# Row maxima and sums of an attention kernel: partition groups joined by scalar copies and a vector transpose instead of a TensorE transpose

## The chip, the cores and the metric

The kernel runs on one core of one Trainium2 chip. The metric is the device time of one execution in microseconds (us), the median of several runs. The core has TensorE (PE, matrix products; PEld is its weight load), VectorE (DVE), ScalarE (ACT), GpSimd (POOL) and SyncE (SP), which here only issues DMAs. Each engine runs its own instructions in order; they wait for each other by semaphores.

## The reference

```python
xn = layernorm(x)                                  # x: 2048 x 640
q  = (xn @ wq) in 32 heads of 128
s  = softmax(q @ k.T * 128**-0.5) @ v              # the last 512 keys of a cache, per head
s  = (heads side by side) @ wo                     # 2048 x 640
h  = relu(xn @ w1 + b1) ** 2                       # 640 -> 1728
g  = silu(h @ w2 + b2)
out = x + s * g
```

All is float32. Products are made from a high and a low part of each operand (fp32r), three matmuls for each product.

## The kernel before, in words

The 2048 rows are four tiles of 512. First the gate `g` is computed for three of the tiles (lines up to about 350; roughly the first 300 us). Then attention runs in 128 **units**: 32 heads times 4 row tiles. The gate of the last tile is mixed into the first and last units.

In a unit the scores lie transposed: keys on the 128 partitions, the 512 rows of x along the free dimension, in four chunks of 128 keys (`KC`), two chunks to a PSUM tile `s` of 128x1024. A unit goes through these steps:

- `s_mm`: 12 matmuls give the scores, in two tiles `s`. There are two such buffers, so the next unit's scores wait until this unit's have been read.
- `max_fold`: VectorE reads 128x1024 scores, transposes each square of 32x32 and takes the maximum over 32 keys (`fold`, group `rdm<-s`). Afterwards partition 32a + i holds maxima over the 32 keys of partition group a, for row 32b + i in column b, for each of the four chunks: 128x64.
- `gather` (`r1m<-rdm`): the maximum over the chunks, 128x16. `turn` (`ptm`): a TensorE transpose against the identity, to a PSUM tile of 16x128. `row` (`rowm<-ptm`): the maximum over the four partition groups a, now along the free dimension, 16x32: one value for each of the 512 rows. Then two DMAs from SP's queue: the row to DRAM (`m_d<-rowm`, 2 KB) and back to all 128 partitions (`bm<-m_d`, 256 KB).
- `shift` (`e<-s,bm`): scores less maxima, on VectorE; this frees the two `s` buffers. `expo` and `p_hi` on ScalarE, `p_lo` and `s_add` on GpSimd: the exponentials, their split in two parts (`pt`), and the sum of the two halves (`su`).
- `s_fold`, `gather`, `turn`, `row` once more for the sums (`rds`, `r1s`, `pts`, `rows`, a reciprocal, `s_d`, `bs`), one unit later.
- `v_mm` (`o<-pt,wv`, 12 matmuls), `o_norm` (times the reciprocal, `o<-o,bs`), `o_hi` and `o_lo` (`ot`). After two heads, `r_mm` (15 matmuls a unit on average) and `r_acc` (`acc<-r,acc`) for the projection by `wo`. `q_mm` (`pq`, 15 matmuls), `q_hi` and `q_lo` make the q of two units ahead. `prep` splits the weights.

The order of the work is written out by hand: a plan gives every step a time within its unit, steps are sorted by these times, and that is the order of the instructions on every engine. The times are used for nothing else.

```python
PERIOD = 12.4
for when, k, f, a in sorted(plan, key=lambda e: e[:2]):
    f(*a)
```

`late_square` squares the activations of the last tile's gate on GpSimd; three of its calls, in the first three units, are planned in the loop over `range(FA, FC)`.

Of the kernel before, what the change touches and what calls it, by code (L numbers as in the profile page):

```python
# [20 lines left out]
def kernel(  # L21
# [21 lines left out]
    FC = (F + P - 1) // P  # L43
    KC = W // P
# [7 lines left out]
    cpool = ctx.enter_context(tc.tile_pool(name="const", bufs=1))  # L52
    dpool = ctx.enter_context(tc.tile_pool(name="dram", bufs=1, space=bass.MemoryType.DRAM))

    ident = cpool.tile([P, P], F32, name="ident")
# [8 lines left out]
    class Ordered:  # L64
# [13 lines left out]
    pe, dve, act, pool, sp = (  # L78
        Ordered(e) for e in (nc.tensor, nc.vector, nc.scalar, nc.gpsimd, nc.sync)
    )  # L80
# [18 lines left out]
    psx = ctx.enter_context(tc.tile_pool(name="psx", bufs=1, space=PSUM))  # L99

    FA = FC - 3
# [76 lines left out]
    def ln_rows(t, mv, xs):  # L178
        pm = psx.tile([P, NT], F32, tag="x", name=f"pmv{t}")
        nc.tensor.transpose(pm[: 2 * NB, :P], mv.rearrange("p a b -> p (a b)"), ident)  # L180
        row = xp.tile([2 * NB, P], F32, tag="lr", name=f"lr{t}", bufs=1)
        nc.vector.tensor_copy(row, pm[: 2 * NB, :P])
        d = dpool.tile([2, NT], F32, name=f"mv_d{t}")
        nc.sync.dma_start(d.rearrange("a (b p) -> (a b) p", p=P), row)
        bc = []
        for i in range(2):
            m = xp.tile([P, D], F32, tag="mr", name=f"mr{t}_{i}")[:, :NT]
            nc.sync.dma_start(m, d[i : i + 1, :].to_broadcast([P, NT]))
            bc.append(m)
        return bc, xs  # L190
# [136 lines left out]
    def mlp_step(n):  # L327
# [47 lines left out]
    PERIOD = 12.4  # L375
    B32 = 32
    AHEAD = 2
    NQ = NT // B32
# [4 lines left out]
    XT, ACC, KT, VV, WQ, WO, Q, E, SC, MB, RD, PT, PO, OT, RB, QPS, FX, CL, PRS, RAW = (  # L383
        {} for _ in range(20)
    )
# [82 lines left out]
    def fold(rd, k, src, op):  # L468
        dve.tensor_reduce(
            rd[:, k * NQ * 2 : (k + 1) * NQ * 2],  # L470
            src.rearrange("p c (b i) -> p (c b) i", i=B32),
            axis=AX.X,
            op=op,
            apply_transpose=True,
        )

    def max_fold(i, k):
        if k == 0:
            RD[i, "m"] = ap.tile([P, KC * NQ], F32, tag="rd", name=f"rdm{i}", bufs=3)
        fold(RD[i, "m"], k, SC[i, k], ALU.max)  # L480

    def gather(i, what):
        rd = RD.pop((i, what))
        n = rd.shape[1] // NQ
        r1 = ap.tile([P, NQ], F32, tag="r1", name=f"r1{what}{i}", bufs=4)
        dve.tensor_reduce(
            r1,
            rd.rearrange("p (c b) -> p b c", b=NQ),
            axis=AX.X,
            op=ALU.max if what == "m" else ALU.add,  # L490
        )
        RD[i, what] = r1

    def turn(i, what):
        pm = psx.tile([P, NT], F32, tag="x", name=f"pt{what}{i}")
        pe.transpose(pm[:NQ, :P], RD.pop((i, what)), ident)
        RD[i, what] = pm

    def row(i, what):
        pm = RD.pop((i, what))  # L500
        r = ap.tile([NQ, B32], F32, tag="row", name=f"row{what}{i}", bufs=4)
        dve.tensor_reduce(
            r,
            pm[:NQ, :P].rearrange("p (a i) -> p i a", i=B32),
            axis=AX.X,
            op=ALU.max if what == "m" else ALU.add,
        )
        if what == "s":
            dve.reciprocal(r, r)
        d = dpool.tile([NQ, B32], F32, tag=f"{what}_d", name=f"{what}_d{i}", bufs=4)  # L510
        sp.dma_start(d, r)
        bc = ap.tile([P, NT], F32, tag=f"b{what}", name=f"b{what}{i}", bufs=2)
        sp.dma_start(bc, d.rearrange("a b -> (a b)")[None, :].to_broadcast([P, NT]))
        (MB if what == "m" else RB)[i] = bc
# [25 lines left out]
        pool.tensor_tensor(RD[i, "su"], E[i, 0], E[i, 1], op=ALU.add)  # L540

    def s_fold(i):
        RD[i, "s"] = ap.tile([P, 2 * NQ], F32, tag="rd", name=f"rds{i}", bufs=3)
        fold(RD[i, "s"], 0, RD.pop((i, "su")), ALU.add)

    def v_mm(i, c):
        hf, g, t, h = units[i]
# [75 lines left out]
    LW, LH, LPH, LPY, LR = {}, {}, {}, {}, {}  # L623
# [98 lines left out]
        else:  # L722
            act.activation(r, ph, AF.Relu, bias=bias)

    def late_square(f):
        pool.tensor_tensor(LR[f], LR[f], LR[f], op=ALU.mult)

    def late_split(f):
        n = chunks[f][1]
# [83 lines left out]
    ap = ctx.enter_context(tc.tile_pool(name="at", bufs=2))  # L813
    pools["psb"] = ctx.enter_context(tc.tile_pool(name="psb", bufs=1, space=PSUM))

    plan = []

    def at(when, f, *a):
        plan.append((max(when, 0.0), len(plan), f, a))
# [16 lines left out]
    for t in range(TPH):  # L836
        for c in range(DC):
            k, late = divmod(c + 1 - t, 2)
# [17 lines left out]
    for i in range(NU):  # L856
        t0 = i * PERIOD

        def on(when, f, *a):
            at(t0 + when, f, *a)  # L860

        hf, g, t, h = units[i]
        for c in range(KC):
            on(0.68 * c, s_mm, i, c)
        if i + AHEAD < NU:
            q_at = 3.45 if i % G and i > UPG else 4.3
            for c in range(DC):
                on(q_at + 0.68 * c, q_mm, i + AHEAD, (c,))
            on(q_at + 3.5, q_hi, i + AHEAD)
            on(q_at + 4.1, q_lo, i + AHEAD)  # L870
        on(1.4, max_fold, i, 0)
        on(2.8, max_fold, i, 1)
        on(3.95, gather, i, "m")
        on(5.0, turn, i, "m")
        on(5.4, row, i, "m")
        on(10.4, shift, i, 0)
        on(11.6, shift, i, 1)
        on(11.7, expo, i, 0)
        on(12.7, p_hi, i, 0)
        on(13.8, expo, i, 1)  # L880
        on(14.8, p_hi, i, 1)
        on(13.9, p_lo, i, 0)
        on(16.2, s_add, i)
        on(PERIOD + 6.2, s_fold, i)
        on(PERIOD + 7.4, gather, i, "s")
        on(PERIOD + (8.45 if i < FC - FA - 1 else 9.2), turn, i, "s")
        on(PERIOD + 9.6, row, i, "s")
        on(18.6, p_lo, i, 1)
        for c in range(KC):
            on(PERIOD + 8.5 + 0.68 * c, v_mm, i, c)  # L890
        on(2 * PERIOD + 4.2, o_norm, i)
        on(2 * PERIOD + 4.9, o_hi, i)
        on(2 * PERIOD + 5.5, o_lo, i)
        if i % G == G - 1:
            for d in range(DC):
                last = i == NU - G - 1
                if i < NU - 1:
                    for when, js in (R_AT_END if last else R_AT)[d]:
                        on(when, r_mm, i, d, js, (R_BANK_END if last else R_BANK)[d])
                    on(when + 0.68 * len(js), r_acc, i, d)  # L900
                if g == NG - 1 and hf == 0:
                    w = (NU // 2 + 9 + 4 * (t * DC + d)) * PERIOD
                    for k, n in enumerate("sxg"):
                        at(w + k * PERIOD - 0.6, load_finish, n, 0, t, d)
                    at(w + 3 * PERIOD - 0.7, finish, 0, t, d)
# [10 lines left out]
    for item in order:  # L916
        kind, n = item[0], int(item[1:] or 0)
# [37 lines left out]
    for f, u in sorted(UP_AT.items()):  # L955
        at(LOAD.get(f, PREP.get(f - 2, 0) + 0.9), late_load, 1, f)
        when = PREP.setdefault(f, u - 5.0)
        at(when, late_prep, 1, f)
        for c in range(DC):
            at(u + 0.68 * c, late_up, f, UP_BANK[f] if f < len(UP_BANK) else (f + 1) % 2, c)  # L960
        relu, square, split = STEPS_AT.get(f, (u + 3.5, u + 4.3, u + 5.7))
        at(relu, late_relu, f, "kv"[f % 2])
        at(square, late_square, f)
        at(split, late_split, f)
# [8 lines left out]
    for k, f in enumerate(range(FA, FC)):  # L973
        t0 = k * PERIOD
        for c in range(DC):
            at(t0 + 8.0 + 0.1 * c, early_up, f, 0, c)
        at(t0 + 10.6, late_relu, f, "s")
        at(t0 + 12.0, late_square, f)
        at(t0 + PERIOD + 7.6, early_split, f)
    at(z + 2.0, late_x)  # L980
    for d in range(DC):
# [51 lines left out]
```

## Time and profile before

| | us |
|---|---|
| median of 3 runs | 2020.71 (2017.9 to 2021.19) |
| profiled execution | 2021.47 |
| its span in the trace | 2019.7 |
| granted TensorE clock | 0.999 of full speed |

In the trace every line of this part of the kernel carries the number of one helper (L72), so instructions are told apart by the names of what they write and read: `rdm<-s` writes `rdm` and reads `s`. A row of a timeline has start, length, engine, operation, and in brackets the idle time before it and what ended it. A group has the busy time in all, the mean in ns of one, and the idle time before. SPq is the sequencer that issues DMAs from SP.

### The profile page before, as it was taken

The page shows a single profiled execution, that of the slowest core. Times are in us where ns is not written, and L with a number is a line of the kernel's source. Part 1 is how long each engine was busy: PE and PEld are TensorE (multiplying, and loading weights), DVE is VectorE, ACT ScalarE, POOL GpSimd, SP SyncE. Part 2 cuts the span into 40 slices and gives each one's busy share as a digit, 9 for nine tenths or more (in the row PEclk, how much of TensorE's full clock was granted, in tenths as well). Part 3 has the DMA queues.
Part 4 walks back from the last instruction along what each step waited for, and adds up shares of the span by engine and source line. Part 5 has one row for each costly group of instructions (what it writes and reads, how often), then busy time and mean ns, then how long its engine had stood idle before and what let it go on. Part 6 is the DMA issues. An engine that isn't in the chain of part 4 may idle for free.

```text
span 2019.7 us, 25025 instructions
## 1 busy us (share of the span) xinstructions
PE 1987.9 (98%) x8832; PEld 1609.3 (80%) x8832; DVE 1535.8 (76%) x2252; ACT 985.8 (49%) x1266; POOL 1375.4 (68%) x754
## 2 busy tenths in 40 slices
PE   7999999999999999999999999999999999999998
PEld 6788887788888888888887788787878888788877
DVE  5532337788888888888887778888888888888864
ACT  4432335555555555555554455555555555555533
POOL 1121227788777777777777788788888888877841
PEclk9999999999999999999999999999999999999999
DMA  4431454322333332333335433333333333333344
GB/s 140 128 113 29 177 196 132 99 90 89 90 89 89 90 89 90 90 91 90 91 96 159 154 95 105 110 110 111 110 110 111 110 112 110 96 91 90 106 146 140
DMA packets 126862, 220.32 MB, mean 109 GB/s; under 512 B 21542, under 2 KB 36304, under 8 KB 125456
## 3 DMA queue, kind: packets, MB, share of 16 engines
q1 hardware_dynamic: 123744, 204.28, 33.6%
q0 software_dynamic: 2992, 14.43, 1.8%
q8 instruction: 70, 1.15, 0.2%
q14 instruction: 56, 0.46, 0.1%
HBM read 194.26 MB, written 24.39 MB: 108 GB/s over the span
## 4 chain that ended last, share of the span: by engine, by line
PE 88%; DMA 6%; DVE 2%; POOL 1%; ACT 1%; issue 1%; SPq 0%; POOLq 0%; DVEq 0%
PE pq L72 20%; PE r L72 19%; PE s L72 17%; PE o L72 15%; DMA bm<-m_d 2%; PE py L96 2%; PE py L97 2%; PE py L95 2%; PE ph L96 2%; PE ph L95 2%; PE ph L97 2%; PE ly L72 2%; DMA m_d<-rowm 1%; PE lu L72 1%; DMA w1r<-in_w_dram 1%; DVE e L72 1%
## 5 line engine op out<-in xcount | busy, mean ns | idle before, releaser
L72 POOL TENSOR_TENSOR pt<-e,pt 128x1024 fp32r<-128x1024 f32 x256 | 617.5, 2412 | 296.1 <-ACT pt L72 296.1
L72 PE MATMUL r<-ot,wo 128*128 128x512 f32 x1920 | 496.9, 389 | 0.5 <-DVE acc L72 0.5
L72 PE MATMUL pq<-ax,wq 128*128 128x512 f32 x1920 | 473.1, 396 | 0.1
L72 ACT ACTIVATE e<-e 128x1024 f32<-128x1024 f32 x256 | 269.5, 1053 | 370.6 <-DVE e L72 331.6
L72 PEld LDWEIGHTS r<-ot,wo 128*128 128x128 f32 x1920 | 360.2, 188 | 75.9 <-DVE acc L72 0.9
L72 PEld LDWEIGHTS pq<-ax,wq 128*128 128x128 f32 x1920 | 350.9, 188 | 84.5 <-DMA ax<-xT_d 0.9
L72 PE MATMUL o<-pt,wv 128*128 128x512 f32 x1536 | 386.5, 398 | 0.4 <-POOL pt L72 0.3
L72 PE MATMUL s<-q,wk 128*128 128x512 f32 x1536 | 372.2, 391 | 9.1 <-DVE e L72 9.0
L72 DVE TRANSPOSE_TENSOR_REDUCE rdm<-s 128x32 f32<-128x1024 f32 x256 | 319.3, 1249 | 60.6 <-PE s L72 46.3
L72 PEld LDWEIGHTS s<-q,wk 128*128 128x128 f32 x1536 | 286.4, 188 | 76.9 <-DVE e L72 16.3
L72 PEld LDWEIGHTS o<-pt,wv 128*128 128x128 f32 x1536 | 278.7, 188 | 70.8 <-POOL pt L72 1.5
L72 DVE TENSOR_TENSOR e<-s,bm 128x1024 f32<-128x1024 f32 x256 | 299.9, 1212 | 37.5 <-DMA bm<-m_d 33.7
L72 POOL TENSOR_TENSOR su<-e,e 128x1024 f32<-128x1024 f32 x128 | 308.5, 2410 | 0.0
L72 ACT ACTIVATE pt<-e 128x1024 fp32r<-128x1024 f32 x256 | 271.7, 1061 | 7.8
L72 DVE TENSOR_TENSOR acc<-r,acc 128x512 f32<-128x512 f32 x300 | 202.5, 675 | 2.8 <-PE r L72 2.8
L237 POOL TENSOR_TENSOR r<-r 128x512 f32<-128x512 f32 (+1 forms) x42 | 44.1, 1049 | 227.5 <-ACT r L278 207.9
L72 ACT ACTIVATE ot<-o 128x512 fp32r<-128x512 f32 x128 | 76.8, 600 | 228.3 <-DVE o L72 228.3
L72 DVE TRANSPOSE_TENSOR_REDUCE rds<-su 128x32 f32<-128x1024 f32 x128 | 158.5, 1239 | 10.7 <-POOL su L72 9.0
L72 ACT ACTIVATE q<-pq 128x512 fp32r<-128x512 f32 x128 | 76.7, 599 | 164.8 <-PE pq L72 164.7
L72 DVE TENSOR_TENSOR ot<-o,ot 128x512 fp32r<-128x512 f32 x128 | 88.5, 691 | 32.0 <-ACT ot L72 32.0
L239 DVE TENSOR_TENSOR h<-r,h 128x512 fp32r<-128x512 f32 (+1 forms) x42 | 29.0, 690 | 107.7 <-ACT h L238 107.6
L72 POOL TENSOR_TENSOR wq<-qr,wq 128x640 fp32r<-128x640 f32 x62 | 98.5, 1588 | 4.0 <-ACT wq L72 2.8
(122 smaller groups left out, 2152.6 us busy)
## 6 DMA issues: line engine op xcount, KB each, us to landing
bm<-m_d SPq DMA_DIRECT2D x128, 256.0 KB, 3.3
bs<-s_d SPq DMA_DIRECT2D x128, 256.0 KB, 4.0
qr<-in_wq_dram SPq DMA_DIRECT2D x64, 320.0 KB, 4.4
or<-in_wo_dram SPq DMA_DIRECT2D x64, 320.0 KB, 4.5
kr<-in_kT_dram SPq DMA_DIRECT2D x64, 256.0 KB, 4.4
vr<-in_v_dram SPq DMA_DIRECT2D x64, 256.0 KB, 4.3
xT_d<-xT POOLq DMA_DIRECT2D x6, 1280.0 KB, 7.5
xb<-in_x_dram SPq DMA_DIRECT2D x16, 320.0 KB, 3.5
```

The lines of the kernel that those rows point to most:

```text
L72: ins = method(*args, **kwargs)
L95: nc.tensor.matmul(ps, ah, bh, start=first and i == 0, stop=False)
L96: nc.tensor.matmul(ps, ah, bl, start=False, stop=False)
L97: nc.tensor.matmul(ps, al, bh, start=False, stop=last and i == n - 1)
L237: nc.gpsimd.tensor_tensor(r, r, r, op=ALU.mult)
L239: nc.vector.tensor_tensor(lo, r, raw(hi), op=ALU.subtract)
```

## The change

The two steps `turn`, the TensorE transposes, are gone. `gather` now copies, on ScalarE, partition groups 1 to 3 of the folded tile beside group 0, so that all lie in partitions 0 to 31: three copies of 32x64 for the maxima, of 32x32 for the sums. `row` reduces over groups and chunks in one VectorE step to 32x16, written into the left half of a 32x32 square that was zeroed once; for the sums the reciprocal is taken there; a VectorE transpose of the square then gives the 16x32 row. The DMAs are as before. `row` is planned earlier (4.45 for 5.4, and 8.5 for 9.6 within the unit). Three early squares of the last tile's gate move from GpSimd to VectorE.

```diff
+    def fold_tile(what, i):
+        n = (KC if what == "m" else 2) * NQ
+        return ap.tile([P, P // B32, n], F32, tag=f"rd{what}", name=f"rd{what}{i}", bufs=2)
...
     def gather(i, what):
-        rd = RD.pop((i, what))
-        n = rd.shape[1] // NQ
-        r1 = ap.tile([P, NQ], F32, tag="r1", name=f"r1{what}{i}", bufs=4)
-        dve.tensor_reduce(
-            r1,
-            rd.rearrange("p (c b) -> p b c", b=NQ),
-            axis=AX.X,
-            op=ALU.max if what == "m" else ALU.add,
-        )
-        RD[i, what] = r1
-
-    def turn(i, what):
-        pm = psx.tile([P, NT], F32, tag="x", name=f"pt{what}{i}")
-        pe.transpose(pm[:NQ, :P], RD.pop((i, what)), ident)
-        RD[i, what] = pm
+        rd = RD[i, what]
+        for a in range(1, P // B32):
+            act.activation(rd[:B32, a, :], rd[a * B32 : (a + 1) * B32, 0, :], AF.Copy)
 
     def row(i, what):
-        pm = RD.pop((i, what))
-        r = ap.tile([NQ, B32], F32, tag="row", name=f"row{what}{i}", bufs=4)
-        dve.tensor_reduce(
-            r,
-            pm[:NQ, :P].rearrange("p (a i) -> p i a", i=B32),
-            axis=AX.X,
-            op=ALU.max if what == "m" else ALU.add,
-        )
+        rd = RD.pop((i, what))[:B32].rearrange("p a (c b) -> p b (a c)", b=NQ)
+        sq = SQ[what, i % 2]
+        dve.tensor_reduce(sq[:, :NQ], rd, axis=AX.X, op=ALU.max if what == "m" else ALU.add)
         if what == "s":
-            dve.reciprocal(r, r)
+            dve.reciprocal(sq[:, :NQ], sq[:, :NQ])
+        r = ap.tile([B32, B32], F32, tag="row", name=f"row{what}{i}", bufs=4)
+        dve.transpose(r, sq)
+        r = r[:NQ]
         d = dpool.tile([NQ, B32], F32, tag=f"{what}_d", name=f"{what}_d{i}", bufs=4)
         sp.dma_start(d, r)
...
-    def late_square(f):
-        pool.tensor_tensor(LR[f], LR[f], LR[f], op=ALU.mult)
+    def late_square(f, eng=pool):
+        eng.tensor_tensor(LR[f], LR[f], LR[f], op=ALU.mult)
...
+    SQ = {
+        (what, k): cpool.tile([B32, B32], F32, name=f"sq{what}{k}") for what in "ms" for k in range(2)
+    }
+    for sq in SQ.values():
+        pool.memset(sq, 0.0)
...
         on(3.95, gather, i, "m")
-        on(5.0, turn, i, "m")
-        on(5.4, row, i, "m")
+        on(4.45, row, i, "m")
...
-        on(PERIOD + 7.4, gather, i, "s")
-        on(PERIOD + (8.45 if i < FC - FA - 1 else 9.2), turn, i, "s")
-        on(PERIOD + 9.6, row, i, "s")
+        on(PERIOD + 8.0, gather, i, "s")
+        on(PERIOD + 8.5, row, i, "s")
...
-        at(t0 + 12.0, late_square, f)
+        at(t0 + 12.0, late_square, f, dve)
```

More of the change, by code (lines that the diff above doesn't have):

```diff
@@ L475, in fold @@
         )
+    def fold_tile(what, i):
+        n = (KC if what == "m" else 2) * NQ
+        return ap.tile([P, P // B32, n], F32, tag=f"rd{what}", name=f"rd{what}{i}", bufs=2)
     def max_fold(i, k):
         if k == 0:
-            RD[i, "m"] = ap.tile([P, KC * NQ], F32, tag="rd", name=f"rdm{i}", bufs=3)
-        fold(RD[i, "m"], k, SC[i, k], ALU.max)
+            RD[i, "m"] = fold_tile("m", i)
+        fold(RD[i, "m"][:, 0, :], k, SC[i, k], ALU.max)
     def gather(i, what):
-        rd = RD.pop((i, what))
-        n = rd.shape[1] // NQ
-        r1 = ap.tile([P, NQ], F32, tag="r1", name=f"r1{what}{i}", bufs=4)
-        dve.tensor_reduce(
-            r1,
-            rd.rearrange("p (c b) -> p b c", b=NQ),
-            axis=AX.X,
-            op=ALU.max if what == "m" else ALU.add,
-        )
-        RD[i, what] = r1
-    def turn(i, what):
-        pm = psx.tile([P, NT], F32, tag="x", name=f"pt{what}{i}")
-        pe.transpose(pm[:NQ, :P], RD.pop((i, what)), ident)
-        RD[i, what] = pm
-    def row(i, what):
-        pm = RD.pop((i, what))
-        r = ap.tile([NQ, B32], F32, tag="row", name=f"row{what}{i}", bufs=4)
-        dve.tensor_reduce(
-            r,
-            pm[:NQ, :P].rearrange("p (a i) -> p i a", i=B32),
-            axis=AX.X,
-            op=ALU.max if what == "m" else ALU.add,
-        )
+        rd = RD[i, what]
+        for a in range(1, P // B32):
+            act.activation(rd[:B32, a, :], rd[a * B32 : (a + 1) * B32, 0, :], AF.Copy)
+    def row(i, what):
+        rd = RD.pop((i, what))[:B32].rearrange("p a (c b) -> p b (a c)", b=NQ)
+        sq = SQ[what, i % 2]
+        dve.tensor_reduce(sq[:, :NQ], rd, axis=AX.X, op=ALU.max if what == "m" else ALU.add)
         if what == "s":
-            dve.reciprocal(r, r)
+            dve.reciprocal(sq[:, :NQ], sq[:, :NQ])
+        r = ap.tile([B32, B32], F32, tag="row", name=f"row{what}{i}", bufs=4)
+        dve.transpose(r, sq)
+        r = r[:NQ]
         d = dpool.tile([NQ, B32], F32, tag=f"{what}_d", name=f"{what}_d{i}", bufs=4)
@@ L542, in s_fold @@
     def s_fold(i):
-        RD[i, "s"] = ap.tile([P, 2 * NQ], F32, tag="rd", name=f"rds{i}", bufs=3)
-        fold(RD[i, "s"], 0, RD.pop((i, "su")), ALU.add)
+        RD[i, "s"] = fold_tile("s", i)
+        fold(RD[i, "s"][:, 0, :], 0, RD.pop((i, "su")), ALU.add)
     def v_mm(i, c):
```

## The prediction

> **What bounds the kernel now.** I read the page first, busy shares and then the chain that ended last.
>
> ```profile
> span 2019.7 us, 25025 instructions
> ...
> PE 1987.9 (98%) x8832; PEld 1609.3 (80%) x8832; DVE 1535.8 (76%) x2252; ACT 985.8 (49%) x1266; POOL 1375.4 (68%) x754
> ...
> PE 88%; DMA 6%; DVE 2%; POOL 1%; ACT 1%; issue 1%; SPq 0%; POOLq 0%; DVEq 0%
> ```
>
> TensorE (PE) is the bound, but 6% of the chain is DMA, so something else ends last in places. To see what, I went to the timeline of one unit in the middle of the run, PE first (start, length, engine, operation).
>
> ```profile
> 682.37 2.88 PE L72 MATMUL s<-q,wk 128*128 128x512 f32 x12
> ...
> 685.09 1.52 PE L72 MATMUL r<-ot,wo 128*128 128x512 f32 x6
> ...
> 687.81 0.27 PE L72 MATMUL ptm<-ident,r1m 128*16 128x128 f32 x1
> ...
> 687.84 2.30 PE L72 MATMUL pq<-ax,wq 128*128 128x512 f32 x9
> ...
> 689.98 0.84 PE L72 MATMUL r<-ot,wo 128*128 128x512 f32 x3
> ...
> 694.86 2.88 PE L72 MATMUL s<-q,wk 128*128 128x512 f32 x12
> ```
>
> From one unit's scores to the next is 694.86 - 682.37 = 12.49 us. Twelve matmuls go out in 685.09 - 682.37 = 2.72 us, 0.2267 each. A unit has 54 of them (15 for q, 12 scores, 12 for P.V, 15 for the output projection): 12.24 us. The other 0.25 us are the unit's two transposes. One can be read: 689.98 - 687.81 = 2.17 us hold nine matmuls (2.04) and `ptm`, so it takes 0.13 us of PE time, though its record says 0.27.
>
> The other ring in a unit runs over VectorE (DVE) and two DMAs: maxima of the scores, their row to DRAM, its broadcast back, the subtraction that frees the score banks. The same unit on DVE, ScalarE (ACT) and the DMA queue (SPq):
>
> ```profile
> 683.93 2.61 DVE L72 TRANSPOSE_TENSOR_REDUCE rdm<-s 128x32 f32<-128x1024 f32 x2 [0.31 <-PE s L72]
> ...
> 685.12 1.06 ACT L72 ACTIVATE pt<-e 128x1024 fp32r<-128x1024 f32 x1
> ...
> 686.57 0.27 DVE L72 TENSOR_REDUCE r1m<-rdm 128x16 f32<-128x64 f32 x1
> ...
> 686.75 0.68 DVE L72 TENSOR_TENSOR acc<-r,acc 128x512 f32<-128x512 f32 x1
> 687.35 0.69 DVE L72 TENSOR_TENSOR o<-o,bs 128x512 f32<-128x512 f32 x1
> ...
> 688.08 0.60 ACT L72 ACTIVATE ot<-o 128x512 fp32r<-128x512 f32 x1 [1.90 <-DVE o L72]
> 688.12 0.28 DVE L72 TENSOR_REDUCE rowm<-ptm 16x32 f32<-16x128 f32 x1
> 688.42 0.33 SPq L72 DMA_DIRECT2D m_d<-rowm  x1
> ...
> 689.76 0.33 SPq L72 DMA_DIRECT2D bm<-m_d  x1
> ...
> 693.15 2.36 DVE L72 TENSOR_TENSOR e<-s,bm 128x1024 f32<-128x1024 f32 x2 [0.17 <-DMA bm<-m_d]
> ...
> 696.42 2.61 DVE L72 TRANSPOSE_TENSOR_REDUCE rdm<-s 128x32 f32<-128x1024 f32 x2 [0.32 <-PE s L72]
> ...
> 698.96 0.65 DVE L72 TENSOR_TENSOR acc<-r,acc 128x512 f32<-128x512 f32 x1
> ```
>
> From the first fold to the end of `rowm`: 688.40 - 683.93 = 4.47 us. From there to `e`: 4.75 us here, and `e` waited for the DMA. The fold that follows at 696.42 waited 0.32 us for PE, so this unit was PE's. A unit whose broadcast came late shows the ring when it alone decides:
>
> ```profile
> 520.73 2.61 DVE L72 TRANSPOSE_TENSOR_REDUCE rdm<-s 128x32 f32<-128x1024 f32 x2 [0.60 <-PE s L72]
> ...
> 524.92 0.28 DVE L72 TENSOR_REDUCE rowm<-ptm 16x32 f32<-16x128 f32 x1 [0.23 <-PE ptm L72]
> ...
> 530.85 2.36 DVE L72 TENSOR_TENSOR e<-s,bm 128x1024 f32<-128x1024 f32 x2 [1.07 <-DMA bm<-m_d]
> ...
> 533.83 2.61 DVE L72 TRANSPOSE_TENSOR_REDUCE rdm<-s 128x32 f32<-128x1024 f32 x2
> ```
>
> Fold to fold 13.10 us: 4.47 to the end of `rowm`, 5.65 to `e`, 2.98 to the next fold, which no longer waits. So the ring takes 7.45 us + d, d being the time from the end of `rowm` to `e`. It decides where d is over 5.04. At the 4.75 of the unit above it takes 12.20: only 0.29 us hide it behind PE's 12.49, and it is just under the 12.24 that PE needs without transposes. This near tie is the whole question. The waits agree that the DMA is late now and then (us in total, times, longest):
>
> ```profile
> DVE e L72 <- DMA bm<-m_d: 33.7, 49, 2.6
> ```
>
> I read d in every unit but the first four and the last, whose surroundings differ: 123 pairs of `rowm` and `e` rows, from the first to the last of these:
>
> ```profile
> 362.48 0.27 DVE L72 TENSOR_REDUCE rowm<-ptm 16x32 f32<-16x128 f32 x1
> ...
> 367.33 2.36 DVE L72 TENSOR_TENSOR e<-s,bm 128x1024 f32<-128x1024 f32 x2 [0.37 <-DMA bm<-m_d]
> ...
> 1901.32 0.28 DVE L72 TENSOR_REDUCE rowm<-ptm 16x32 f32<-16x128 f32 x1
> ...
> 1906.20 2.36 DVE L72 TENSOR_TENSOR e<-s,bm 128x1024 f32<-128x1024 f32 x2
> ```
>
> 77 have d up to 4.72, 24 lie between 4.72 and 5.04 (mean 4.85), and 22 are over 5.04 (mean 5.63): those are the ring's already.
>
> **The change part by part.** Durations of the groups (total busy, then mean ns of one, then idle before):
>
> ```profile
> L72 DVE RECIPROCAL rows<-rows 16x32 f32<-16x32 f32 x128 | 43.7, 341 | 4.4
> ...
> L72 PE MATMUL ptm<-ident,r1m 128*16 128x128 f32 x128 | 34.7, 271 | 1.4 <-DVE r1m L72 1.1 <-issue 0.3
> L72 DVE TENSOR_REDUCE r1m<-rdm 128x16 f32<-128x64 f32 x128 | 33.0, 258 | 2.4
> ...
> L72 DVE TENSOR_REDUCE r1s<-rds 128x16 f32<-128x32 f32 x128 | 24.1, 188 | 4.4
> ...
> L72 DVE TENSOR_TENSOR mv<-sc 128x4 f32<-128x4 f32 x4 | 0.6, 162 | 0.1
> ...
> L72 ACT ACTIVATE wk<-kr 128x512 fp32r<-128x512 f32 x64 | 39.8, 622 | 0.0
> ...
> L154 ACT ACTIVATE sc<-sc 128x4 f32<-128x4 f32 x4 | 0.8, 206 | 2.0 <-DVE sc L72 1.9
> ...
> L72 ACT ACTIVATE e<-e 128x1024 f32<-128x1024 f32 x256 | 269.5, 1053 | 370.6 <-DVE e L72 331.6 <-POOL wk L72 17.1 <-POOL wo L72 15.5
> ```
>
> *PE.* All 256 transposes go. At 0.125 us each that is 32 us, the most the change can give; PE then needs 12.24 us a unit.
>
> *Scalar copies.* Three a join, two joins a unit. From 206 ns at 4 elements and 622 at 512 a copy of 64 is about 255 ns, one of 32 about 230 (estimates). The fold of the maxima ends 2.61 us after its start; ACT takes over 0.04 us later (as `ot` at 688.08 followed `o`, ended at 688.04), and three copies are done at 2.61 + 0.04 + 0.77 = 3.42. ACT is free then: its `pt` ended at 686.18, 2.25 after the fold began. In the changed order DVE runs `acc` and `o` right behind the folds: `acc` goes out 2.54 after the first fold (698.96 - 696.42), `o` 0.60 later (as at 686.75 and 687.35), the joined maximum 0.60 after that, at 3.75. So the copies are hidden, with 0.3 us to spare; without that cover the first 0.3 us cost nothing and each further us costs a us in every unit where the ring decides. Behind them on ACT stand `ot`, which needs `o` anyway, and, behind those of the sums, the weight copies and then the exponentials, before which ACT waits 331.6 us for DVE, 2.6 us a unit: covered.
>
> *The joined reduction.* It reads 256 elements in each of 32 partitions where `r1m` read 64 in 128. At the rate of one element per 0.96 ns that 162 ns for 4 and 188 for 32 give, it is 0.40 us; at the slope from `r1s` to `r1m` (70 ns for 32 elements) 0.68. I take 0.55, the middle, since neither row is near.
>
> The Trainium skill (SBUF - State Buffer, in "Door 1: The DMA port swizzle") has a rule that speaks against this step: SBUF is read in 16-byte lines, and each access in a new line pays a penalty. The elements here lie 64 bytes apart, each in a line of its own. The trace is divided: `r1s` has the same spacing and shows no penalty, `r1m` does. By the rule the sum would be that of the second rival below.
>
> *The turn on VectorE.* 32 elements; no row shows it. It is nearest to `r1s` (188 ns for 32), bounded by 162 and 258: I take 0.20. So `rowm` ends at 3.75 + 0.55 + 0.03 (the gap from `rdm` to `r1m`) + 0.20 = 4.53 instead of 4.47, rounded up with one hand-over more to 0.07 later. With the bounds, 0.13 earlier to 0.25 later.
>
> *The sums.* The same steps, half as wide, off the ring: in the 4.75 us until `e` DVE has `ot`, `q` and at most one more `acc` (0.60 each), a fold (1.30), the join (0.4), a reciprocal (under the 0.34 of 32 elements, it has 16) and the turn (0.2): 4.04. Nothing. The sums' row no longer waits for its place among PE's matmuls, so its two DMAs are issued earlier; they stand behind `bm` on SPq as before.
>
> *Sum.* The ring becomes 7.52 + d. In the 77 units d is at most 4.72, so PE decides: 0.25 each, 19.2 us. In the 24 the period is 7.52 + 4.85 = 12.37, a gain of 0.12 each, 2.9. The 22 late ones lose 0.07 each, 1.5. Together 20.6. The other five units: 1.25 for their transposes and the 1.4 us that PE stood idle before `ptm`, less about 0.5 for each of the first two units, where no `acc` or `o` hides the copies: 1.6. The three early squares that go from GpSimd to DVE I cost at nothing: in the new order each falls before folds that wait for PE, 0.67 us in this row, as long as a square of the size of `acc` takes; uncovered they would be some 2 us.
>
> ```profile
> 332.94 1.25 DVE L72 TRANSPOSE_TENSOR_REDUCE rdm<-s 128x32 f32<-128x1024 f32 x1 [0.67 <-PE s L72]
> ```
>
> 22 us off the profiled execution's 2021.47 us gives 1999.3; that execution is 0.8 above the median of 2020.71, so 1998.5 in its terms; I say 1999.
>
> **The rivals.**
>
> *PE decides nearly everywhere.* If the reduction takes 0.40 us, `rowm` ends 0.05 earlier than now or better, and 90 or more units run at 12.24: 25 to 31 us gained, 1989 to 1995. For it speaks `r1s`; against it, d itself must not grow.
>
> *The ring swallows half of the gain.* With 0.68 us and a turn of 0.2, `rowm` ends 0.20 later; only 32 units have room for PE's 12.24, 69 gain little, and 11 us remain: about 2009. For it speaks the slope to `r1m`. This is what the skill's rule on lines would make of it. Near 0.3 later the gain is used up: no change.
>
> *Slower: the copies are not hidden.* Were they 0.5 us each, hand-overs counted, the join could start only at 2.61 + 0.04 + 1.5 + 0.03 = 4.18, `rowm` would end about 0.5 later, and every unit would be the ring's: some 24 us lost, about 2045. It decides from about 0.43 us a copy. Against it: 206 ns for the smallest ACT row. For it: none of the rows reads one group of partitions and writes another.
>
> The skill (ScalarE: Activation LUTs, "What ACT_TABLE_LOAD costs") gives 186 ns + 0.833 ns an element and says that back-to-back ones overlap by 93 ns; the 622 ns at 512 agree, and three copies would then be some 0.5 us, not 0.77.
>
> That the transposes stay can't be: none is issued any more.
>
> **How the numbers follow.** Forecast (1995 to 2005) 0.45, PE nearly everywhere 0.20, half swallowed (2005 to 2016) 0.18, no change 0.05, slower 0.12. Within 0.2%, 4 us, this kernel can't be told from no change. Faster is 0.45 + 0.20 + 0.18 = 0.83. The range takes in the first three cases, 1989 to 2017, and leaves out the rest.
>
> **What would show it.** Right: PE-bound units 12.24 us apart; `rowm` ending 4.5 to 4.6 after the first fold; the joined maximum not waiting for ACT; more waits of `e` for `bm` (33.7 us in 49 now would rise), for the slack is gone. Wrong: a joined maximum that waits for ACT, or over 0.7 us of reduction; units at 12.4 or more with folds that never wait for PE; a longer d, if the sums' DMAs get in the way of `bm`.

## The result and the profile after

| | before | changed kernel |
|---|---|---|
| median of 4 runs each | 2019.87 us (2017.9 to 2021.19) | 1997.3 us (1995.06 to 1998.71) |
| ratio to before | | 0.9887 [0.9876, 0.9899] |
| profiled execution | 2021.47 | 1995.06 |
| its span | 2019.7 | 1993.3 |

Forecast was 1999. The page of the changed kernel: busy time of the engines, the chain that ended last, and the two groups of scalar copies.

```profile
span 1993.3 us, 25531 instructions
...
PE 1961.8 (98%) x8576; PEld 1601.6 (80%) x8576; DVE 1563.8 (78%) x2255; ACT 1183.6 (59%) x2034; POOL 1374.1 (69%) x755
...
PE 87%; DMA 5%; DVE 4%; POOL 1%; ACT 1%; issue 1%; SPq 0%; DVEq 0%; ACTq 0%; POOLq 0%
...
L72 ACT ACTIVATE rdm<-rdm 32x64 f32<-32x64 f32 x384 | 98.2, 256 | 38.2 <-DVE rdm L72 33.4
L72 ACT ACTIVATE rds<-rds 32x32 f32<-32x32 f32 x384 | 87.6, 228 | 49.4 <-DVE rds L72 45.1
```

PE has 256 instructions fewer (8832 to 8576) and is as full as before. DVE's share of the chain went from 2 to 4%: the second ring is nearer. The copies take 256 and 228 ns.

The medians differ by 22.6 us, this pair of traces by 26.4, since the traced execution of the kernel before is above all four of the table and that of the changed one is the lowest of its four. To see where the 26.4 us of span came from I cut it at the first folds of the fifth and of the last unit, which leaves the 123 periods, from fold to fold, that the prediction counted (worked out from the starts of the folds `rdm<-s`):

| us | before | after | gain |
|---|---|---|---|
| up to the first counted fold | 357.92 | 358.16 | -0.2 |
| 123 periods | 1551.7 | 1525.4 | 26.3 |
| from the last counted fold on | 110.08 | 109.75 | 0.3 |
| PE's floor for them (123 x 12.49, x 12.24) | 1536.3 | 1505.5 | 30.8 |
| over the floor | 15.4 | 19.9 | -4.5 |

So all of it lies in the units: PE gave 30.8 us, and the ring of DVE and DMAs took 4.5 back. The size of the second part hangs on the execution. A second trace of the changed kernel stands 18.7 us over the floor, near the 19.9 here, but the two experiments below that add only a few idle transposes at the start of the kernel before stand 9.9 over it, not 15.4. Two neighbouring units in the timeline of the changed kernel (start, length, engine, operation):

```profile
677.63 3.01 PE L72 MATMUL s<-q,wk 128*128 128x512 f32 x12 [0.36 <-DVE e L72]
...
679.30 2.63 DVE L72 TRANSPOSE_TENSOR_REDUCE rdm<-s 128x32 f32<-128x1024 f32 x2
...
680.48 1.52 PE L72 MATMUL r<-ot,wo 128*128 128x512 f32 x6
...
681.97 0.79 ACT L72 ACTIVATE rdm<-rdm 32x64 f32<-32x64 f32 x3 [0.19 <-DVE rdm L72]
682.04 0.69 DVE L72 TENSOR_TENSOR acc<-r,acc 128x512 f32<-128x512 f32 x1
682.65 0.69 DVE L72 TENSOR_TENSOR o<-o,bs 128x512 f32<-128x512 f32 x1
683.25 0.58 DVE L72 TENSOR_REDUCE sqm<-rdm 32x16 f32<-32x256 f32 x1
683.86 0.20 DVE L72 STREAM_TRANSPOSE rowm<-sqm 32x32 f32<-32x32 f32 x1
...
688.74 2.35 DVE L72 TENSOR_TENSOR e<-s,bm 128x1024 f32<-128x1024 f32 x2 [1.05 <-DMA bm<-m_d]
...
691.77 2.63 DVE L72 TRANSPOSE_TENSOR_REDUCE rdm<-s 128x32 f32<-128x1024 f32 x2
...
694.32 0.65 DVE L72 TENSOR_TENSOR acc<-r,acc 128x512 f32<-128x512 f32 x1
694.43 0.79 ACT L72 ACTIVATE rdm<-rdm 32x64 f32<-32x64 f32 x3 [0.18 <-DVE rdm L72]
...
695.49 0.57 DVE L72 TENSOR_REDUCE sqm<-rdm 32x16 f32<-32x256 f32 x1
696.10 0.20 DVE L72 STREAM_TRANSPOSE rowm<-sqm 32x32 f32<-32x32 f32 x1
```

Three things are to be seen. First, the copies are hidden: they are over at 681.97 + 0.79 = 682.76, 3.46 after the first fold, while DVE is with `o` until 683.34. Second, the two units differ. In the lower one `acc` goes out 694.32 - 691.77 = 2.55 after the first fold, and the row is done at 4.53. In the upper one `acc` starts at 2.74: the six `r` matmuls, whose sum it adds, end only at 680.48 + 1.52 = 682.00. The row is done at 4.76. Third, the ring decides here: the fold at 691.77 has no idle time before it, it comes 12.47 us after the one before, and PE's scores ahead of the first fold waited 0.36 us for `e`.

Over all counted units the row ends 4.74 after the first fold in one half of the units and 4.52 in the other (medians), where it was 4.47 before, and the median periods are 12.39 and 12.27. Only 54 of 123 periods are at most 0.03 over PE's floor, which is called on the floor below; before it was 95.

The joined row's instructions in the changed kernel, one tile at a time (shortest, median, longest in ns, first and last start), with what the reduction of the maxima waited for (us, times), and for the sums:

```profile
L72 DVE TENSOR_REDUCE sqm<-rdm x128: 564/578/617, 311.6 to 1887.3; 32x16 f32<-32x256 f32 x128
L72 DVE STREAM_TRANSPOSE rowm<-sqm x128: 198/199/202, 312.2 to 1887.9; 32x32 f32<-32x32 f32 x128
...
  ACT rdm L72: 5.8, 11
```

```profile
L72 DVE TENSOR_REDUCE sqs<-rds x128: 342/360/379, 329.0 to 1906.4; 32x16 f32<-32x128 f32 x128
L72 DVE RECIPROCAL sqs<-sqs x128: 240/241/244, 329.4 to 1906.7; 32x16 f32<-32x16 f32 x128
```

And the wait that answers to the 33.7 us in 49 of before (us, times, longest):

```profile
DVE e L72 <- DMA bm<-m_d: 99.2, 125, 3.2
```

Now `e` waits for its broadcast in nearly every unit. Yet d, from the row's end to `e`, went over 5.04 in 6 of 123 units and no longer in 22. The prediction took d as given; this had to be explained.

### The profile page after: what moved, and what is told of

The parts are those of the page before. It is cut to its first block, busy times and chain, and to the rows that moved or that the text cites. A ratio compares the mean times of both kernels' runs of the same rounds, so it can differ in the third digit from the quotient of the medians.

```text
span 1993.3 us, 25531 instructions
## 1 busy us (share of the span) xinstructions
PE 1961.8 (98%) x8576; PEld 1601.6 (80%) x8576; DVE 1563.8 (78%) x2255; ACT 1183.6 (59%) x2034; POOL 1374.1 (69%) x755
## 3 DMA queue, kind: packets, MB, share of 16 engines
q1 hardware_dynamic: 123744, 204.28, 33.7%
## 4 chain that ended last, share of the span: by engine, by line
PE 87%; DMA 5%; DVE 4%; POOL 1%; ACT 1%; issue 1%; SPq 0%; DVEq 0%; ACTq 0%; POOLq 0%
PE r L72 20%; PE pq L72 20%; PE s L72 17%; PE o L72 16%; PE ly L72 2%; PE py L96 2%; PE py L97 2%; PE py L95 2%; PE ph L96 2%; PE ph L97 2%; PE ph L95 2%; DMA bm<-m_d 2%; PE lu L72 1%; DMA w1r<-in_w_dram 1%; DMA m_d<-rowm 1%
## 5 line engine op out<-in xcount | busy, mean ns | idle before, releaser
L72 PE MATMUL pq<-ax,wq 128*128 128x512 f32 x1920 | 456.5, 389 | 1.6 <-DMA ax<-xT_d 1.5
L72 PEld LDWEIGHTS pq<-ax,wq 128*128 128x128 f32 x1920 | 360.3, 188 | 77.0 <-DMA ax<-xT_d 2.3
L72 DVE TENSOR_TENSOR e<-s,bm 128x1024 f32<-128x1024 f32 x256 | 301.5, 1219 | 99.3 <-DMA bm<-m_d 99.2
L72 PE MATMUL o<-pt,wv 128*128 128x512 f32 x1536 | 372.1, 390 | 1.4 <-POOL pt L72 0.9
L72 DVE TRANSPOSE_TENSOR_REDUCE rdm<-s 128x32 f32<-128x1024 f32 x256 | 318.9, 1248 | 38.8 <-PE s L72 19.5
L72 PEld LDWEIGHTS o<-pt,wv 128*128 128x128 f32 x1536 | 287.2, 188 | 65.6 <-POOL pt L72 6.1
L72 ACT ACTIVATE rdm<-rdm 32x64 f32<-32x64 f32 x384 | 98.2, 256 | 38.2 <-DVE rdm L72 33.4
L72 ACT ACTIVATE rds<-rds 32x32 f32<-32x32 f32 x384 | 87.6, 228 | 49.4 <-DVE rds L72 45.1
```

The source lines that it names most:

```text
L72: ins = method(*args, **kwargs)
```

## Experiments

Results are given by the median and by the ratio to the kernel before, run on the same chip in the same rounds. "Periods" are the 123 of the table above, and a late row is one whose first DMA (`m_d`) and second (`bm`) are issued over 1.5 us apart. Before had 25 late rows, the changed kernel 7.

**Is the gain PE's time?** The transposes come back, as idle ones that no row waits for.

```diff
+    def turn(i, what):
+        pm = psx.tile([P, NT], F32, tag="x", name=f"pt{what}{i}")
+        pe.transpose(pm[:NQ, :P], ident[:, :NQ], ident)
...
+        on(5.0, turn, i, "m")
...
+        on(PERIOD + (8.45 if i < FC - FA - 1 else 9.2), turn, i, "s")
```

> The changed kernel with the 256 TensorE transposes put back at their old places in PE's order, now of a piece of the identity and read by nobody: PE's time as before, the row's way as after. Theory (PE's time is most of the gain, and rows that arrive late cost more when PE's floor is low): PE needs 12.49 us a unit again, the DVE-DMA ring at 4.53 or 4.76 + 2.98 us + the DMA time of some 4.4 to 4.7 us stays under that, so units run at 12.49 and only a few late ones longer: about 2015 us, +18 on the changed kernel, and some 5 us under the kernel before, because fewer rows come late. Rival (the gain is PE's time alone): 2020, no difference to the kernel before. Rival (the gain is the earlier DMAs of the sums, PE's time is hidden anyway): 2000 or less.

Measured 2015.26 us, ratio 0.998 [0.997, 0.9989]: some 18 of the 22.6 us are gone. Two folds in its timeline and the idle transpose between them:

```profile
686.24 2.61 DVE L72 TRANSPOSE_TENSOR_REDUCE rdm<-s 128x32 f32<-128x1024 f32 x2 [0.33 <-PE s L72]
...
690.12 0.27 PE L72 MATMUL ptm<-ident 128*16 128x128 f32 x1
...
698.73 2.61 DVE L72 TRANSPOSE_TENSOR_REDUCE rdm<-s 128x32 f32<-128x1024 f32 x2 [0.19 <-PE s L72]
```

The folds are 12.49 apart again and wait for PE. 110 of 123 periods are on that floor, though the row ends as late as in the changed kernel (4.74 and 4.51) and no row waits for the transposes. So the gain is the 0.125 us of PE time of each transpose, not the shorter way of the row. The 4 us that stay go with the late rows: 8 here, 25 before, and 6.2 us over the floor where before had 15.4. In the trace of the kernel before, 15.1 of these 15.4 us stand in the 25 periods with a late row.

**Is the rest of the floor held back by the row's end?** `acc` goes behind the row instead of in front of it.

```diff
+                done = when + 0.68 * len(js)
+                if not last and 3.0 < done % PERIOD < 4.5:
+                    done += 4.6 - done % PERIOD
-                on(when + 0.68 * len(js), r_acc, i, d)
+                on(done, r_acc, i, d)
```

> The changed kernel with the output sums (acc) that stand between the folds and the joined maximum on DVE moved behind the row of maxima. Theory (in every second unit acc waits for PE's projection matmuls and holds the joined maximum back, 4.76 us from fold to row instead of 4.53, and the ring decides there): the joined maximum then starts when the three copies are done, 3.48 after the first fold, and the row ends at 4.29 in both kinds of unit; ring 4.29 + 2.98 + d under 12.24 for every d up to 4.97, so all but the late units run at PE's 12.24: 10 to 15 us less than the changed kernel, 1983 to 1987. Rival (the ring is not what holds units at 12.4, but DVE's total work): the same work in another order, no change, 1997. The wait of the joined maximum for ACT should now appear in most units, 0.3 us each.

Measured 1984.74 us, ratio 0.9825 [0.9806, 0.9843], against 0.9887 for the change as it is. DVE in its timeline, and the wait that appeared:

```profile
679.72 2.61 DVE L72 TRANSPOSE_TENSOR_REDUCE rdm<-s 128x32 f32<-128x1024 f32 x2 [0.29 <-PE s L72]
...
682.25 0.67 DVE L72 TENSOR_TENSOR o<-o,bs 128x512 f32<-128x512 f32 x1
...
683.18 0.59 DVE L72 TENSOR_REDUCE sqm<-rdm 32x16 f32<-32x256 f32 x1 [0.27 <-ACT rdm L72]
683.81 0.20 DVE L72 STREAM_TRANSPOSE rowm<-sqm 32x32 f32<-32x32 f32 x1
683.95 0.64 DVE L72 TENSOR_TENSOR acc<-r,acc 128x512 f32<-128x512 f32 x1
...
691.96 2.61 DVE L72 TRANSPOSE_TENSOR_REDUCE rdm<-s 128x32 f32<-128x1024 f32 x2 [0.32 <-PE s L72]
```

```profile
DVE sqm L72 <- ACT rdm L72: 34.7, 126, 1.0
```

The row ends at 4.30 in both halves of the units, 102 of 123 periods are on the floor of 12.24, and the folds wait for PE. The copies now show, by 0.27 us each, and it does not matter. So the changed kernel's loss against PE's floor is a matter of where the row ends, and 0.2 to 0.4 us of that was one accumulation that stood in front of it.

**What if the copies were not hidden?** The three copies of the maxima are made twice: the rival that ended on the other side.

```diff
-        for a in range(1, P // B32):
+        for a in (1, 2, 3) * (2 if what == "m" else 1):
```

> The changed kernel with the three scalar copies of each maximum made twice, six of 0.256 us. Theory (three are hidden behind acc and o, by 0.3 us, and beyond that each us costs a us in the units where the ring decides): the copies end about 2.65 + 1.55 + 0.03 = 4.23 us after the first fold, the joined maximum starts 0.3 to 0.5 us later than now, every unit is the ring's at 12.6 to 12.7: about +30 us, 2024 to 2034, slower than the kernel before. Rival (ACT has time to spare, 59% busy, and the copies stay hidden): within 5 us of 1997.

Measured 2060.46 us, ratio 1.0199 [1.0181, 1.0217]: 63 us over the changed kernel, about twice what I expected. The direction holds, the size was wrong: the ring had been put at 12.6 to 12.7 us, and the first four units took 6 us longer than in the changed kernel besides. Its chain of what ended last, and one unit:

```profile
PE 38%; DMA 26%; DVE 20%; ACT 11%; issue 3%; POOL 2%; SPq 0%; ACTq 0%; DVEq 0%
```

```profile
700.76 2.61 DVE L72 TRANSPOSE_TENSOR_REDUCE rdm<-s 128x32 f32<-128x1024 f32 x2
703.40 1.66 ACT L72 ACTIVATE rdm<-rdm 32x64 f32<-32x64 f32 x6 [0.15 <-DVE rdm L72]
705.09 0.58 DVE L72 TENSOR_REDUCE sqm<-rdm 32x16 f32<-32x256 f32 x1 [0.31 <-ACT rdm L72]
705.71 0.20 DVE L72 STREAM_TRANSPOSE rowm<-sqm 32x32 f32<-32x32 f32 x1
...
710.58 2.35 DVE L72 TENSOR_TENSOR e<-s,bm 128x1024 f32<-128x1024 f32 x2 [1.29 <-DMA bm<-m_d]
...
713.61 2.61 DVE L72 TRANSPOSE_TENSOR_REDUCE rdm<-s 128x32 f32<-128x1024 f32 x2
```

This is the ring alone: row at 5.15, 4.67 to `e`, 3.03 to the next fold, 12.85 us, the median of the units, and 123 x 12.85 = 1581 of the 1583.0 us of its periods. No unit is PE's. It shows how a ring that is off the chain today becomes the chain whole: 0.41 us more on the row in one half of the units, 0.63 in the other, and PE's share of the chain falls from 87 to 38%.

**What does the spacing of the joined reduction cost?** The fold writes in another order, so that the four chunks of a column lie side by side (16 bytes) instead of 64 bytes apart; the copies carry the order along.

```diff
-            rd[:, k * NQ * 2 : (k + 1) * NQ * 2],
-            src.rearrange("p c (b i) -> p (c b) i", i=B32),
+            rd.rearrange("p (b c) -> p c b", b=NQ)[:, 2 * k : 2 * k + 2, :],
+            src.rearrange("p c (b i) -> p c b i", i=B32),
...
-        rd = RD.pop((i, what))[:B32].rearrange("p a (c b) -> p b (a c)", b=NQ)
+        rd = RD.pop((i, what))[:B32].rearrange("p a (b c) -> p b a c", b=NQ)
...
-        dve.tensor_reduce(sq[:, :NQ], rd, axis=AX.X, op=ALU.max if what == "m" else ALU.add)
+        dve.tensor_reduce(sq[:, :NQ], rd, axis=AX.XY, op=ALU.max if what == "m" else ALU.add)
```

> The changed kernel with the folded tile laid out so that the four chunks' maxima of a row block are neighbours (the fold writes with a stride, the copies are unchanged in size): the joined reduction reads runs of 16 bytes (8 for the sums) instead of single elements 64 bytes apart. By the Trainium skill's rule on SBUF lines of 16 bytes (SBUF - State Buffer, Door 1: The DMA port swizzle) the reduction should fall from 0.578 us to about 0.40 (162 ns and 0.97 ns an element), the row ends 0.17 earlier, and the ring of the units at 12.4 comes under PE's 12.24: some 8 us less, 1989. Rival (the time goes with the number of elements reduced to one, not with their distance): 0.578 stays, 1997; the fold, writing with a stride, may even be slower than 1.25.

Measured 1986.68 us, ratio 0.9842 [0.9821, 0.9863]. The same tiles as above, and the fold:

```profile
L72 DVE TENSOR_REDUCE sqm<-rdm x128: 385/396/410, 312.8 to 1879.2; 32x16 f32<-32x256 f32 x128
```

```profile
L72 DVE TENSOR_REDUCE sqs<-rds x128: 252/273/277, 330.6 to 1897.7; 32x16 f32<-32x128 f32 x128
```

```profile
L72 DVE TRANSPOSE_TENSOR_REDUCE rdm<-s x256: 1205/1251/1255, 309.3 to 1876.8; 128x32 f32<-128x1024 f32 x128
```

The same 256 elements take 396 ns instead of 578, and the sums' 128 take 273 instead of 360, while the fold that now writes with a stride is as long as before (1251, mean 1248 in the changed kernel). The row ends at 4.55 and 4.33, 90 periods are on the floor. The rule of the Trainium skill that the prediction weighed (SBUF - State Buffer, "Door 1: The DMA port swizzle") agrees with this: elements each in its own 16-byte line cost 182 ns over 256 of them, 0.7 ns each. Why `r1s`, with the same spacing and 188 ns for 32 elements, showed nothing of it in the kernel before, no run tells. In the prediction's range of 0.40 to 0.68, the lower bound is the packed reduction, and the true 0.578 lies near the middle that was taken for want of a nearer row; that part of the hit is luck.

**Which half brings what, and whose are the late rows?** Once only the maxima are made the new way, once only the sums. My theory was that the sums' row, whose DMAs are issued earlier, leaves the queue free for the maxima.

```diff
 maxima only:
-        on(PERIOD + 8.0, gather, i, "s")
-        on(PERIOD + 8.5, row, i, "s")
+        on(PERIOD + 7.4, gather_pe, i, "s")
+        on(PERIOD + (8.45 if i < FC - FA - 1 else 9.2), turn, i, "s")
+        on(PERIOD + 9.6, row_pe, i, "s")
 sums only:
-        on(3.95, gather, i, "m")
-        on(4.45, row, i, "m")
+        on(3.95, gather_pe, i, "m")
+        on(5.0, turn, i, "m")
+        on(5.4, row_pe, i, "m")
```

`gather_pe`, `turn` and `row_pe` are the steps of the kernel before.

> One half of the change: the maxima go the new way, the sums the old one (with their TensorE transposes at the old place and their row at its old time). PE needs 12.365 us a unit. Theory (in the kernel before, many maxima rows land late because the weight loads, issued behind the sums' row and its broadcast, are still under way; the change issues the sums' row about 1 us earlier): with the sums the old way the late rows are back, 20 or more units with over 5.04 us from row to subtraction instead of 6, and each of them costs about 0.9 us: 2010 to 2018. Rival (rows come late for another cause, and the change removed that with the maxima's own transposes): under 10 late rows, 2002 to 2006.

> The other half: the sums go the new way, the maxima the old one with their TensorE transposes. PE needs 12.365 us a unit, the ring of DVE and DMAs is the old one, 4.47 us from fold to row and 12.1 to 12.2 in all at the usual DMA time. Theory (early sums keep the rows from being late, and the new way of the maxima costs the ring 0.05 to 0.29 us): under 12 late rows, nearly every unit at 12.365, about 2000 (1997 to 2003), within 5 us of the whole change although half of the transposes remain. Rival (lateness has another cause): 20 or more late rows, 2008 or more.

Measured 2008.35 us, ratio 0.9931 [0.9914, 0.9948], with the maxima alone, and 2010.96, 0.9949 [0.9934, 0.9964], with the sums alone: 12.3 and 9.7 us, together 22.0 of the change's 22.6. The theory about the queue fell: with the maxima alone 8 rows are late, with the sums alone 36. (The time with the maxima alone lies between the two ranges expected for it, so there the count decides and not the time.) The time from the `m_d` issue to its landing (least, median, greatest, in us), in the answers for `m_d` of the first and of the second:

```profile
DMA to landing us min/median/max: 1.3/1.3/4.2
```

```profile
DMA to landing us min/median/max: 1.3/1.9/3.6
```

The lateness belongs to the old way of the maxima, over PE: the idle transposes above, for which no row waits, left 8. What goes on in such a row is seen in the DMA view of the kernel before, over the 2.4 us of the late unit of the prediction and, below it, over those of a unit on time (queues with packets, MB and share of the 16 engines; then the DMA issued, with the us to landing):

```profile
q8 instruction: 1, 0.02, 3.1%
...
m_d<-rowm SPq DMA_DIRECT2D x1, 2.0 KB, 2.4
```

```profile
q1 hardware_dynamic: 32, 0.00, 1.4%
...
m_d<-rowm SPq DMA_DIRECT2D x1, 2.0 KB, 1.3
```

In the late unit a 16 KB packet of an instruction queue, q8, runs while the 32 small packets of the row are under way. I take q8 for PE's: it has 70 packets before and 68 after, for 17,664 and 17,152 matmuls and weight loads, one for about every 256. I counted the meetings for all rows (a packet of q8, or of the other instruction queue, q14, with packets of 8 KB, under way 0.3 to 1.3 us after the issue of `m_d`; in brackets those with one of q8):

| kernel | late rows with such a packet | rows on time with one |
|---|---|---|
| before | 21 of 25 (19) | 0 of 98 |
| sums only | 33 of 36 (32) | 2 of 87 |
| changed | 4 of 7 (4) | 2 of 116 |
| maxima only | 5 of 8 (1) | 2 of 115 |

The count in the expectation of the next experiment, 21 and 33 packets of 16 KB, is thus that of both queues. The traces say more than that the two meet. In all 32 of these rows of the sums alone, and in 18 of the 19 before, the second DMA (`bm`) is issued 1.04 to 1.20 us after the packet of q8 ends, whether that is 0.4 or 1.7 us after the issue of `m_d`: when the row lands goes by the end of the packet. This makes the packet the likely cause; no run took the packets away, so it is not shown beyond that.

**Does the packet meet the row by chance?** If it did, shifting PE's instructions by some should move the count. Before got 7, then 14 idle transposes at its start.

```diff
+    def idle_turns():
+        pm = psx.tile([P, NT], F32, tag="x", name="idle")
+        for _ in range(7):
+            pe.transpose(pm[:NQ, :P], ident[:, :NQ], ident)
...
+    at(0.0, idle_turns)
```

> The kernel before, with seven idle transposes in front of the attention on PE: 14 more instructions (weight load and matmul each), 0.9 us, nothing else. In the traces so far the rows of maxima that take over 1.5 us to DRAM are many (25 and 36 of 123) in the two kernels whose maxima go through PE, and 21 and 33 of these have a 16 KB packet of PE's instruction queue under way at the same time, none or two of the others. PE fetches 256 instructions at a time, about every 2.2 units, so in a unit the fetches fall about 28 instructions (3 us) apart, always near the same places. Theory (chance of phase): shifted by 14 instructions the fetches miss the rows, under 12 late ones, 4 to 8 us less than the kernel before: 2012 to 2016. Rival (the fetch comes when PE reaches the transpose, or late rows have another cause that the coincidence follows): 20 or more late rows, 2019 to 2023.

> The same with fourteen idle transposes, 28 instructions, 1.8 us. Theory (chance of phase): shifted by about one whole distance the fetches meet the rows again, 15 or more late ones, 2019 to 2024. Rival: as with seven, whatever that gave, plus 1 us.

Measured 2018.38 and 2019.58 us, ratios 1.0004 [0.9994, 1.0014] and 1.0006 [0.9997, 1.0016]; 20 and 19 late rows, 18 of them with a packet in each. The theory of chance fell: the meetings stay when the order is shifted. In these kernels many packets of q8 crowd into the last microsecond before `m_d`'s issue (19 of 55 in the kernel before); where the maxima don't pass through PE they come mostly 1 to 3 us ahead of it. They follow the transposes: 37 of the 55 start within 1 us after a transpose, of maxima or of sums, has started, 37 and 38 in the two shifted kernels, but 15 of 54 where the transposes are idle ones. Why PE is fetching just then stays open.

**Are the moved squares free?** They go back to GpSimd in the changed kernel. The first result was too near the changed kernel to settle it, so the edit ran again beside it.

```diff
-        at(t0 + 12.0, late_square, f, dve)
+        at(t0 + 12.0, late_square, f)
```

> The changed kernel with the three early squares back on GpSimd. Theory (they are hidden on either engine): within 1 us of the changed kernel, 1996 to 1998. Rival (GpSimd bounds the first units, where it has no idle time, and each square of 1.04 us delays the sums there): 1999 to 2001.

> The changed kernel itself, beside the next one on the same chip: 1996 to 1999.

> The changed kernel with the three early squares on GpSimd, beside the changed kernel on the same chip. Theory (hidden on either engine, and 2001 was the chip or the phase of the first units): within 1 us of it. Rival (GpSimd bounds the first units): 2 to 4 us more than it.

Measured 2001.15 (0.99 [0.9885, 0.9915]), then 1996.09 (0.9889 [0.9874, 0.9904]) beside 1998.33 (0.99 [0.9884, 0.9917]) for the changed kernel itself. By the ratios the first is 0.0013 (2.6 us) over the changed kernel of the result, with intervals that overlap; the second is 2.2 us under the one beside it: inconclusive end to end. In the traces the first ten units, from fold to fold, took 124.0 us in both of the changed kernel, and 126.5 and 126.9 with the squares on GpSimd. But that difference lies in the first two units, and there it is not shown to be the squares'. The second unit's scores on PE, in the changed kernel and, below, in the second run with the squares on GpSimd:

```profile
318.65 3.00 PE L72 MATMUL s<-q,wk 128*128 128x512 f32 x12 [2.49 <-DVE e L72]
```

```profile
320.26 5.46 PE L72 MATMUL s<-q,wk 128*128 128x512 f32 x12 [3.17 <-DVE e L72]
```

After the longer wait the same twelve matmuls take 5.46 us, 0.427 apart instead of 0.227, and the clock granted between 322.0 and 325.6 us is 0.50. The broadcast behind that wait took 4.10 us from issue to landing, where it had 3.42. The kernel with the maxima alone has its squares on VectorE and shows the same: a wait of 2.97 us, matmuls 0.427 apart, and first two periods of 14.02 and 13.98 us, where the two runs with squares on GpSimd have 14.2 to 14.3 and 13.8 to 14.2 and the changed kernel 12.3 to 12.7 and 12.9.

**Do the two mends add up?** `acc` behind the row and the packed reduction together.

> The changed kernel with both: acc behind the row of maxima, and the chunks' maxima as neighbours. Theory (either alone brings the ring under PE's 12.24 us in nearly every unit; what is left over is the late rows): the row ends about 4.12 us after the first fold, only units with over 5.14 us from row to subtraction pay, 2 to 4 us less than the better of the two alone: 1980 to 1983. Rival (they gain side by side, 12 + 10 us): 1975.

Measured 1985.45 us, ratio 0.9822 [0.9807, 0.9836]. The row ends at 4.11, 108 periods are on the floor, 7.4 us remain over it, and the time is that of the accumulation's move alone, above both ranges expected. Below 4.3 there is nothing left to win from the row's end: PE's 12.24 and the few late rows are what is left. The move alone and the two together beat the changed kernel by some 12 us.

## Why the prediction was right, point by point

- *PE's time.* 0.25 us a unit, 12.49 to 12.24: held, and shown by the return of the idle transposes (18 of 22.6 us back). The record of 271 ns would have promised twice as much; the spacing of the matmuls around it gave the right price.
- *Copies.* 255 and 230 ns forecast, 256 and 228 measured; done at 3.42 forecast, 3.46 measured. Hidden, as forecast: DVE waited for ACT 11 times in 128. The Trainium skill (ScalarE: Activation LUTs, "What ACT_TABLE_LOAD costs") would have them overlap by 93 ns; these do not, three take 0.79 us.
- *Reduction and turn.* 0.55 and 0.20 forecast, 0.578 and 0.199 measured. The 0.55 was the middle of two bounds and came near by luck. The lower bound has a slip: from 162 ns for 4 elements to 188 for 32 is 0.93 ns an element, not 0.96; it is 0.40 us either way.
- *The row's end: the step that failed.* 4.53 forecast. It is right in one half of the units (4.52). In the other it is 4.74, since `acc` stands in front of the row there and waits for six matmuls, which I had not looked for: I took the start of `acc` from one unit (2.54) and applied it to all. Moving `acc` took it away.
- *d: the other one.* I took it as unchanged, with 22 units over 5.04; it was 6. The late rows were tied to the old way over PE. Before and the kernel with idle transposes have the same floor, and they stand 15.4 and 6.2 us over it: some 9 us, though the row of the second ends later. By the traces of the two shifted kernels, 9.9 over the floor, it is some 4.
- *The two against each other.* The ring was to take back 30.8 - 20.6 = 10.2 us of PE's gain in the counted units and took 4.5. Without the fewer late rows, 4.5 + 9.2 = 13.7 would be the estimate from this pair of traces, because of the 4.74. The errors were of opposite sign: the units gained 26.3 us in this pair, where 20.6 was forecast, beside -0.2 and 0.3 for the head and the tail, for which I had 1.6. By the medians the gain is 22.6, and the forecast was 22. That they agree so closely is in part luck: the row ends later in half of the units than I had it, and fewer rows are late.
- *The head.* 1.6 us forecast, nothing measured; the first four units took 50.1 us instead of 49.7. The step that failed is the price of the copies where nothing hides them. I had about 0.5 us for each of the first two units; the row ends 4.39 us after the fold in both, where it was 3.59 and 3.64, so 0.80 and 0.75 later. The chain that ended last now runs through these rows and their broadcasts, and did not before. That is some 0.5 us of the difference; the rest stays open.
- *Sums.* Cost nothing that shows, as forecast; alone they brought 9.7 us, although 36 rows were late then. *Squares.* Nothing forecast, nothing that can be told apart.
- *What would show it.* Units 12.24 apart: 54 of 123. `rowm` ending at 4.5 to 4.6: in one half of the units. No wait for ACT: nearly so. More waits of `e` for `bm`: 33.7 us to 99.2. Of the rivals, the unhidden copies are a real mechanism (six copies are enough), but a copy takes 0.256 us and not the 0.5 that this rival needed; a ring that swallows half is what the changed kernel does in every second unit, where the median period is 12.39.

## What to carry to other kernels

Where two rings lie within 0.3 us of each other, a saving on the one is worth only what the other leaves: work out both, the second with its DMAs in the loop, and read more than one unit, since neighbours may differ. Before an instruction is shortened, see what stands in front of it on its in-order engine; here moving one accumulation behind the row brought half as much again as the change itself. The length in an instruction's record is not its price: between pipelined matmuls, read it from the distance of the neighbours. One pair of traces gives the parts of a gain no better than single executions agree: here 26.4 us where the medians gave 22.6.

## What the runs showed of the hardware

- A reduction over elements 64 bytes apart: 578 ns for 256 elements in each of 32 partitions, 396 where they lie in runs of 16 bytes; 360 and 273 for 128 elements 64 bytes apart and in runs of 8 bytes. Writing its results 16 bytes apart instead of side by side cost the fold nothing (1251 ns for 1248).
- Small scalar copies from one group of partitions to another (256 and 228 ns) follow one another without overlap: three of the first take 0.79 us, six 1.66.
- A TensorE transpose of 128x16 takes 0.125 us of PE's time, while its record says 0.27.
- A 2 KB DMA that is under way with a 16 KB packet of the instruction queue lands after 1.5 to 2.4 us in most cases (kernel before) instead of 1.3; the packets take about 0.96 us and come about every 28 us, one for about 256 PE instructions.
- In the second unit of six traces PE waited 2.96 to 4.20 us for `e`, and its next matmuls ran 0.427 us apart for a while, at a granted clock down to 0.50; in the other eight, with waits up to 2.90 us there, they ran at 0.227 at once.
